# Reciprocals one product later in couples 6 to 9, and one weight sum in the other half of couple 10

## The chip, the core and the metric

The kernel runs on one core of a Trainium2 chip. Its time is the device time of one launch in microseconds; several launches give a median. The core has TensorE (PE in the profile, with its weight loads as PEld), VectorE (DVE), ScalarE (ACT), GpSimd (POOL) and SyncE (SP), which here only issues copies (DMAs). Each engine works through its own instructions in the order in which they were written; engines wait for each other through semaphores. TensorE writes into PSUM banks, and VectorE or ScalarE must empty a bank before TensorE can write the next result into it.

## The reference

Attention with normalised queries and keys (8 batches, 12 heads, 448 positions, 64 numbers per head) is followed by a feed-forward block with SiLU. All is fp32.

```python
q_n, k_n = rmsnorm(q, g_q), rmsnorm(k, g_k)
scores = matmul(q_n, k_n.T) / sqrt(64)
attn = exp(scores - max(scores)); attn /= sum(attn) + 1e-9
x = matmul(attn, v)            # arranged as 3584 tokens x 768
h = x @ w_in                   # 768 x 2048
out = (h * sigmoid(h)) @ w_out # 2048 x 768
```

## The kernel before, in words

The attention is worked off in 24 *couples* c = 0 to 23, each of two head pairs (four heads) of one batch. `GROUP` is 6 and `LATE` is 12. Each couple has a *visit* and a *between*.

**The visit.** `visit(c)` does the score matmuls of couple c (L712), the exponentials on ScalarE (L717), and the products with the values (`weigh`, L749), which gather unnormalised sums in two PSUM banks, `av0` and `av1`. The end of the weighing of couple c - 1 lies in visit c: after it, `divide(c - 1, sums)` (L808, VectorE) multiplies the two banks by the reciprocals r and writes x. Until that is done, the first `weigh` of couple c cannot start its new sums in these banks.

**The between.** `between(c)` prepares the next couple and, from couple 6 on, does a share of the first feed-forward matmul for the six couples (two batches) finished before. This share is the *filler*. It is dealt in two halves by `fill`: the first before, the second after the transposes of the next keys (L647) and the matmuls that sum the exponentials (L783). In couples 6 to 11 a half is 13 steps of one 128x128 by 128x448 matmul each.

**The filler's products.** The feed-forward matmul uses a seven-product scheme on 2x2 blocks (class `Seven`), with the order 1, 2, 6, 5, 7, 3, 4. A product is three steps into one bank (L907). After it the bank is emptied: products 2, 6, 7, 3 and 4 by a VectorE add (`plus`, L857), products 1 and 5 by a ScalarE copy (L915, L925). Between 7 and 3 GpSimd makes two adds: L927 adds product 5 to the term which product 3's emptying reads, and L928 makes another result. Two banks (`ps_mm`) take turns, so a product needs the bank of the last but one. When a block of seven is done, `activate` runs SiLU on its two rows (L1045, ScalarE) and SP saves them (L940). The generator of a product gives control back after each matmul, so the emptying of a product is written down when the next step is asked for.

**What `fill` interleaves.** `others` are spread evenly over the half's steps: normalising the next but one couple (L467 on ScalarE, L468 and L492 on VectorE, the power L496 on GpSimd), preparing `w_in` (below), and the adds L763 of the exponentials. `prompt` is a list with times of its own: its first entry is written before the first step, each further one after three more steps, which is one product. In the second half the prompt entries are the two halves of the reciprocal of the sums: `invert(0)`, and `invert(1)` with `spread`, L792 on VectorE. `spread` issues six copies on SP: four L799, then two L801, which overwrite what the first read and so wait until these have landed. They bring the reciprocals to where `divide` reads them. For couples 3 and 4 an empty entry stands ahead of the two, so that they come one product later.

**Preparing `w_in`.** Its four chunks are taken in pieces: SP loads raw words (L85), ScalarE opens them (L100, L101), VectorE rounds (L123, L126, L130) and GpSimd adds low bits (L134). The next load into a raw buffer waits for L134 of the piece that had it. Each finished chunk also needs four sums (`sum_w_in`, steps 0 to 3, L854 and L857 on tile W), which the products 5, 6, 7 and 3 read as weights. Those of the last chunk stand in the first half of couple 10 (entry 8 of `sums_halves`; the index is twice the couple's distance from `GROUP`, plus the half).

The instructions of each engine stand in the written order; nothing reorders them. SP works off its copies in order too, and one that waits holds up those behind it.

Of the kernel before, what the change touches and what calls it, by code (L numbers as in the profile page):

```python
# [535 lines left out]
def bounded(  # L536
# [13 lines left out]
    GROUP, LATE = z.NPAIR, z.LATE  # L550
# [13 lines left out]
    def piece(n):  # L564
        nonlocal at
        at += n
        return work[:, at - n : at]
# [71 lines left out]
    def transpose_k(c):  # L639


        assert z.KB == BANK
        t = ps.tile([P, 2, BANK], F32, name="sc", bufs=2)
        rows = place[f"k{c % 2}"]
        for i in range(2):
            for j in range(z.KEYS + 1 - i):
                nc.tensor.transpose(t[:, i, ts(j, P)], rows[:, ds((z.KA, z.KB)[i] + j * P, P)], ident)  # L647
        columns = t.rearrange("p i s -> p (i s)")[:, 0 : z.NK]
        nc.scalar.activation(kT, columns, AF.Copy, scale=gains)
        loads["k" if c < LATE - 1 else "quarters"](min(c + 2, LATE))  # L650

    def flip(c, name):

        if name == "q":
            nc.vector.transpose(qT.rearrange("p i s -> p (i s)"), q_of(c)[:, 0 : z.NK])
            load_q(c + 1)
            return
        nc.vector.transpose(kT, place["k1"])
        if c + 1 < NC:
            loads["quarters"](c + 1)  # L660
# [106 lines left out]
    def sum_up(c):  # L767

        n = D // 2
        early = c < GROUP
        t = bank(S) if c < GROUP - 1 else ps.tile([P, 2, BANK], F32, name="sc", bufs=2)[:, 0, 0:S]
        terms = [(0, lambda: weights(c, 0))]
        if early:
            terms = [(0, lambda: weights(c, LEFT - 1))] + terms + [(1, None)]
        for k, (which, w) in enumerate(terms):
            if k == len(terms) - 2:
                yield  # L780
            for h in range(2):
                for i in range(2):
                    nc.tensor.matmul(  # L783
                        t[ds(h * D + i * n, n), :],
                        ones[:, which + i if which else 0],
                        eleft[:, h] if which else w()[:, i, h],
                        start=(k == 0), stop=(k == len(terms) - 1),
                    )

        def invert(half):  # L790
            rows = ts(half, S // 2)
            nc.vector.reciprocal(out=r[0][:, rows], in_=t[:, rows])  # L792

        def spread():
            mine = [a.rearrange("(h i p) s -> i h p s", h=2, i=2) for a in r]
            queues = (nc.sync, nc.gpsimd if c == GROUP - 1 else nc.sync)
            for h in range(2):
                for i in range(2):
                    queues[h].dma_start(mine[1][i, h], mine[0][1, h])  # L799
            for h in range(2):  # L800
                queues[h].dma_start(mine[0][1, h], mine[0][0, h])  # L801

        yield [lambda: invert(0), lambda: (invert(1), spread())]

    def divide(c, source):
        for i in range(2):
            x = x_of(c, i)
            nc.vector.tensor_tensor(  # L808
                out=x, in0=x if source is None else source[i], in1=r[i], op=ALU.mult
            )  # L810
# [148 lines left out]
    def sum_w_in(i, step):  # L959

        assert room.w_in.rounded >= (i + 1) * z.NW
        summed.add((i, step))
        w = room.chunk(i).rearrange("p (c m r k) -> p c m r k", c=z.NW, m=2, r=2)
        up, low = w[:, 0:HW], w[:, HW:]
        s = room.sums(i).rearrange("p (s c m k) -> p s c m k", s=3, c=HW, m=2)
        left_sums(
            up[:, :, :, 0], low[:, :, :, 0], up[:, :, :, 1], low[:, :, :, 1],
            s[:, 0], s[:, 1], s[:, 2], (step,),
        )
# [8 lines left out]
    def sum_x(group, c, steps=range(4)):  # L978
        right_sums(*quarters(group, c), *sums_of_x(c), steps)
# [357 lines left out]
    def fill(others=(), prompt=()):  # L1337


        others, prompt, steps, dealt = list(others), list(prompt), 0, 0  # L1340
        if prompt:
            prompt.pop(0)()
        filler["due"] += filler["share"]
        total = max(1, int(filler["due"] / S))
        while filler["due"] > 0:
            step = next(filler["work"], None)
            if step is None:
                break
            filler["due"] -= step
            steps += 1  # L1350
            if prompt and steps % HW == 0:
                prompt.pop(0)()
            while dealt < min(len(others), len(others) * steps // total):
                others[dealt]()
                dealt += 1
        filler["due"] = min(filler["due"], 0.0)
        for other in prompt + others[dealt:]:
            other()
# [8 lines left out]
    def finish():  # L1367
        run(filler["work"])
# [10 lines left out]
    for c in range(GROUP // 2):  # L1379
        halves[2 * (c - GROUP)], halves[2 * (c - GROUP) + 1] = "rr", "o"  # L1380
    sums_halves = {-6: [(0, 0)], -4: [(0, 1)], -3: [(0, 2)], -2: [(0, 3)]}
    sums_halves[8] = [(3, step) for step in range(4)]
    sums_visits = {GROUP + 1: 1, GROUP + 3: 2}

    def weights_in(c, half):
        i = 2 * (c - GROUP) + half
        work = [step_of[step] for step in halves.get(i, "ro" if c < GROUP else "")]
        return work + [lambda a=a: sum_w_in(*a) for a in sums_halves.get(i, ())]
# [8 lines left out]
    def last_two(c):  # L1397
        return [c // GROUP * 2 - 2, c // GROUP * 2 - 1]
# [63 lines left out]
    def run_all(work):  # L1462
        for piece in work:
            piece()

    def between(c):

        def transposes_and_sums():
            summing = sum_up(c)
            if c < GROUP:  # L1470
                next(summing)
            if c == GROUP - 1:
                reciprocals = next(summing)
                divide(c - 1, None)
                run_all(reciprocals)
                sum_x([0, 1], 0)
                transpose_k(c + 1)
                return
            if c < LATE - 1:
                transpose_k(c + 1)  # L1480
            reciprocals = next(summing)
            if LATE - 1 <= c < NC - 1:
                reciprocals += [lambda: flip(c + 1, "k"), gain]
            if GROUP // 2 <= c < EARLY:
                divide(c - 1, None)
            return reciprocals

        if c < LATE - 1:
            transpose_q(c + 1)
        elif c < NC - 1:  # L1490
            flip(c + 1, "q")
        if c < GROUP // 2:
            inverting.extend(transposes_and_sums())
        elif c == GROUP - 1:
            transposes_and_sums()
        if c >= GROUP and c % GROUP == 0:
            fetched = range(AHEAD) if c == GROUP else ()
            columns = products - 2 * HW * S * len(fetched)
            work = halves_in(last_two(c), range(HF), plain_in, dict(begun), fetched)
            begin(work, columns, 2 * GROUP)  # L1500
            begun.clear()
        late = add(c, LEFT - 1) + add(c, LEFT) if c >= GROUP else []
        further = normalise(c + 2) if c >= GROUP - 1 else []
        fill(late + weights_in(c, 0) + (further[2:] if c >= GROUP else further[:2]))
        prompt = transposes_and_sums() if GROUP // 2 <= c != GROUP - 1 else []
        if prompt and c < GROUP:
            prompt.insert(0, lambda: None)
        if c == GROUP // 2:
            begin(make_ahead([0, 1]), AHEAD * 2 * HW * S, GROUP - 1)
        if c >= LATE - 2:  # L1510
            if c == LATE - 2:
                prompt.append(pair_up)
            queries = prompt[3:] + [lambda: sum_squares(c + 2)]
            fill(weights_in(c, 1), prompt[:3] + [lambda: run_all(queries)])
        else:
            fill(weights_in(c, 1) + (further[:2] if c >= GROUP else []), prompt)
        if c % GROUP == GROUP - 1:
            finish()
            if c == GROUP - 1:
                begun[0] = fetch_ahead([0, 1], 0)  # L1520
            elif c < NC - 1:
                sum_x([c // GROUP * 2, c // GROUP * 2 + 1], 0, range(2))
        if c >= LATE - 2:
            scale(c + 2)
        if GROUP <= c < NC - 1:

            nc.scalar.activation(first, minus_half, AF.Exp)
        if c == NC - 1:
            while rounder.load():
                pass  # L1530
# [238 lines left out]
```

## Time and profile before

| | us |
|---|---|
| median of three launches | 1319.01 (1318.58 to 1319.05) |
| profiled execution, its own time | 1321.49 |
| profiled execution, span | 1319.7 |
| PE busy | 1296.1 |
| DVE busy | 951.2 |
| ACT busy | 505.5 |
| POOL busy | 361.6 |

Couples 6 to 10 lie between about 123 and 297 us of the span. Rows of the timeline give the start in us from the span's start, the duration, the engine, the line and operation, output and inputs, the number of instructions merged, and in brackets how long the engine had stood idle before and what released it. On TensorE each matmul is two records in this profile, so a product of three matmuls is "x6". A duration on TensorE holds the time in the pipeline too: the starts of neighbouring rows say how fast work proceeds.

### The profile page before, as it was taken

Reading aid. Unit: us, or ns where it says so; the run is one execution under the profiler, and the core shown is the slowest. Engines: PE = TensorE matmul, PEld = TensorE weight load, DVE = VectorE, ACT = ScalarE, POOL = GpSimd, SP = SyncE. Lnnn points to the kernel's source line nnn. Section 1 sums busy time; section 2 is a strip of 40 time slices with the busy share of each in tenths; the row PEclk is TensorE's granted clock in tenths of the full one; section 3 lists DMA queues with packets and bytes.
Section 4 is the critical chain, followed back from the end, with each engine's and each line's share of the span. In section 5 each row is a group of like instructions: output and inputs, shape, how many; then the busy total and the mean of one; then the engine's idle time right before and its main releaser. Section 6 shows DMA issues by size and latency. Waiting matters only on the chain.

```text
span 1319.7 us, 19838 instructions
## 1 busy us (share of the span) xinstructions
PE 1296.1 (98%) x7193; PEld 829.9 (63%) x7193; DVE 951.2 (72%) x1629; ACT 505.5 (38%) x886; POOL 361.6 (27%) x230
## 2 busy tenths in 40 slices
PE   8989999999999999999999999999999999999998
PEld 4433444444444444444444455558999999999998
DVE  6888776785755555855554686698978787878785
ACT  7956555654555555454544244410100000000000
POOL 6756533343334333433420244410000000000000
PEclk9999999999999999999999999999999999999999
DMA  8664336333444444444321367412323232231311
GB/s 228 171 174 128 113 91 195 89 90 86 97 103 109 99 93 118 98 93 118 84 64 67 111 201 258 143 60 76 101 76 106 78 100 97 84 117 61 132 45 39
DMA packets 249439, 144.94 MB, mean 110 GB/s; under 512 B 184292, under 2 KB 233220, under 8 KB 249332
## 3 DMA queue, kind: packets, MB, share of 16 engines
q1 hardware_dynamic: 248672, 142.42, 38.6%
q8 instruction: 59, 0.97, 0.3%
q0 software_dynamic: 352, 0.96, 0.2%
q14 instruction: 48, 0.39, 0.1%
q10 hardware_dynamic: 308, 0.20, 0.1%
HBM read 93.98 MB, written 41.29 MB: 102 GB/s over the span
## 4 chain that ended last, share of the span: by engine, by line
PE 87%; DVE 5%; ACT 3%; issue 2%; DMA 2%; POOL 1%; SPq 0%; ACTq 0%; DVEq 0%; POOLq 0%
PE alone L1214 23%; PE mm L907 19%; PE sc L907 9%; PE av L749 8%; PE mm L1214 8%; PE sc L712 8%; PE alone L907 7%; PE alone L1251 2%; PE sc L783 1%; ACT work L717 1%; DMA work<-work 1%; PE mm L1251 1%; DVE work L792 1%; DVE work L763 1%; DMA hidden<-stage 1%
## 5 line engine op out<-in xcount | busy, mean ns | idle before, releaser
L717 ACT ACTIVATE work<-sc,rms 128x448 f32<-128x448 f32 x324 | 185.0, 634 | 70.1 <-PE sc L712 53.5
L907 PE MATMUL mm<-x,W 128*128 128x448 f32 x414 | 169.5, 544 | 3.0 <-DVE stage L857 1.6
L712 PE MATMUL sc<-work 64*64 64x448 f32 x1344 | 165.4, 548 | 1.8 <-ACT work L717 1.5
L763 DVE TENSOR_TENSOR work<-work 128x896 f32<-128x896 f32 (+1 forms) x114 | 123.7, 1118 | 50.7 <-PE av L749 45.4
L749 PE MATMUL av<-work,rows 64*64 64x448 f32 x1296 | 152.8, 541 | 2.9 <-ACT av L725 2.2
L907 PE MATMUL mm<-sums_x,W 128*128 128x448 f32 x372 | 152.5, 543 | 1.9 <-DVE parts L857 1.9
L496 POOL TENSOR_TENSOR rms<-rms,minus_half 128x14 f32<-128x14 f32 (+4 forms) x43 | 105.2, 2449 | 150.6 <-DVE rms L492 140.8
L907 PEld LDWEIGHTS mm<-x,W 128*128 128x128 f32 x414 | 76.6, 190 | 86.2 <-issue 75.5
L523 POOL DMA_DIRECT2D out_dram<-x x2 | 1.2, 594 | 443.3 <-DVE x L857 443.3
L907 PEld LDWEIGHTS mm<-sums_x,W 128*128 128x128 f32 x372 | 69.2, 190 | 75.2 <-issue 67.6
L1214 PE MATMUL alone<-W,rows 128*128 128x192 f32 x610 | 113.0, 326 | 0.0
L749 PEld LDWEIGHTS av<-work,rows 64*64 64x64 f32 x1296 | 57.7, 132 | 75.2 <-issue 34.8
L1214 PEld LDWEIGHTS alone<-W,rows 128*128 128x128 f32 x610 | 101.4, 190 | 0.0
L712 PEld LDWEIGHTS sc<-work 64*64 64x64 f32 x1344 | 53.0, 133 | 75.2 <-ACT work L717 30.7
L927 POOL TENSOR_TENSOR parts<-parts,stage 128x448 f32<-128x448 f32 x31 | 42.1, 1357 | 147.9 <-DVE parts L857 147.7
L907 PE MATMUL sc<-x,W 128*128 128x448 f32 x198 | 80.6, 543 | 0.0
L688 POOL TENSOR_TENSOR rms<-rms,minus_half 128x28 f32<-128x28 f32 x12 | 57.5, 4793 | 61.4 <-DVE rms L685 54.8
L1214 PE MATMUL alone<-W,work 128*128 128x192 f32 x382 | 72.2, 326 | 0.0
L1045 ACT ACTIVATE stage<-stage 128x896 f32<-128x896 f32 x63 | 57.3, 945 | 21.9 <-DVE stage L857 21.1
L1224 ACT COPY rows<-alone 128x192 f32<-128x192 f32 x33 | 10.5, 319 | 142.1 <-PE alone L1214 78.4
L468 DVE TENSOR_REDUCE rms<-rows 128x8 f32<-128x512 f32 (+2 forms) x56 | 35.9, 641 | 39.1 <-ACT rows L467 37.9
L1214 PEld LDWEIGHTS alone<-W,work 128*128 128x128 f32 x382 | 63.8, 190 | 0.0
(258 smaller groups left out, 2276.7 us busy)
## 6 DMA issues: line engine op xcount, KB each, us to landing
hidden<-stage SPq DMA_DIRECT2D x63, 448.0 KB, 3.1
work<-hidden SPq DMA_DIRECT2D x21, 1024.0 KB, 5.0
rows<-in_moe_w_out_dram SPq DMA_DIRECT2D x32, 384.0 KB, 3.4
W<-in_moe_w_in_dram SPq DMA_DIRECT2D x22, 512.0 KB, 5.4
work<-work SPq DMA_DIRECT2D x141, 56.0 KB, 2.0
x<-hidden SPq DMA_DIRECT2D x7, 1024.0 KB, 5.6
rows<-in_q_dram SPq DMA_DIRECT2D x96, 56.0 KB, 2.2
rows<-in_k_dram SPq DMA_DIRECT2D x96, 56.0 KB, 2.2
```

What stands on the lines that cost most here:

```text
L468: nc.vector.tensor_reduce(out=out, in_=t.rearrange("p (n d) -> p n d", n=n), axis=AX.X, op=ALU.add)
L496: nc.gpsimd.tensor_tensor(out=t, in0=t, in1=half, op=ALU.pow)
L688: nc.gpsimd.tensor_tensor(out=f, in0=f, in1=minus_half.to_broadcast([P, n]), op=ALU.pow)
L712: nc.tensor.matmul(two[ds(half * D, D), h, 0:S], keys[rows, ts(half, D)], qT[rows, pair, :], start=True, stop=True,)
L717: nc.scalar.activation(eleft[:, h] if j == LEFT else weights(c, j)[:, i, h], two[:, h, 0:S], AF.Exp, scale=norm.column(c, i, h, j),)
L749: nc.tensor.matmul(sums[i][ds(h * D, D), :], v, w, start=(j == 0 and step == 1), stop=(j == LEFT - 1 and step == 1),)
L763: nc.vector.tensor_tensor(out=total, in0=total, in1=more, op=ALU.add)
L907: nc.tensor.matmul(t, self.left(name, s), self.right(name, s), start=s == ends[0], stop=s == ends[1])
L927: nc.gpsimd.tensor_tensor(out=u2, in0=u2, in1=p5, op=ALU.add)
L1045: nc.scalar.activation(t, t, AF.Silu)
L1214: nc.tensor.matmul(t, x[:, i], y, start=i == ORDER[0], stop=i == ORDER[-1])
L1251: nc.tensor.matmul(o, a[:, 2 * i + m, t], right_one(name, i)[:, m], start=n == 0, stop=n == len(steps) - 1,)
```

## The change

It has three parts.

1. The empty entry ahead of the reciprocals is now put in for couples up to 9 and not only up to 5: `c < LATE - 2` in place of `c < GROUP`. In couples 6 to 9 the first half of the reciprocal is written after the first product's worth of steps of the second half, and the second half, with the spread's copies, after the second.
2. In couple 10 the first half of the filler gets three sums of the last chunk of `w_in`, and the second half the fourth.
3. In couples 10 and 11 the second half's `others` are now this list followed by as many empty entries. In couple 10 the fourth sum is thereby dealt about halfway through; in couple 11 the list is empty, as before.

```diff
-    sums_halves[8] = [(3, step) for step in range(4)]
+    sums_halves[8] = [(3, step) for step in range(3)]
+    sums_halves[9] = [(3, 3)]
...
-        if prompt and c < GROUP:
+        if prompt and c < LATE - 2:
             prompt.insert(0, lambda: None)
...
             queries = prompt[3:] + [lambda: sum_squares(c + 2)]
-            fill(weights_in(c, 1), prompt[:3] + [lambda: run_all(queries)])
+            steps = weights_in(c, 1)
+            fill(steps + [lambda: None] * len(steps), prompt[:3] + [lambda: run_all(queries)])
```

The built programs hold the same instructions. Their order is the same on PE, ACT and POOL. On VectorE, in couples 6 to 9, a product's emptying now precedes the first half of the reciprocal; in couples 6, 7 and 9 the second half follows the rounding of a piece of `w_in` (and in couple 6 another emptying), and in couple 8 it follows product 3's emptying and precedes the rounding. In couple 10 the three emptyings of the first half stand one instruction earlier among the adds L763 and the weight sums. On SP the six copies of the spread move behind a weight load and two saves in couple 6, and behind two saves in couple 9.

## The prediction

> **What bounds the kernel now.** The page comes first: TensorE is busy nearly all of the span, so only stretches in which it stands idle can be won, and each new wait of TensorE costs its full length.
>
> ```profile
> span 1319.7 us, 19838 instructions
> ...
> PE 1296.1 (98%) x7193; PEld 829.9 (63%) x7193; DVE 951.2 (72%) x1629; ACT 505.5 (38%) x886; POOL 361.6 (27%) x230
> ```
>
> The timeline of TensorE gives the start of each couple (the first score matmuls of its visit): couple 7 at 157.43, 8 at 191.65, 9 at 227.22, 10 at 260.54, 11 at 297.23. So the stretches from 7 to 11 take 34.2, 35.6, 33.3 and 36.7 us. The stretch of couple 9 has no idle product and is my measure of "clean". Products elsewhere that start late:
>
> ```profile
> 183.93 4.78 PE L907 MATMUL mm<-x,W 128*128 128x448 f32 x12 [0.62 <-ACT stage L925]
> ...
> 219.85 2.52 PE L907 MATMUL mm<-sums_x,W 128*128 128x448 f32 x6 [1.58 <-DVE parts L857]
> ...
> 281.81 2.52 PE L907 MATMUL mm<-x,W 128*128 128x448 f32 x6 [0.90 <-DVE stage L857]
> ```
>
> A product runs 2.25 us (4.51 between two starts two products apart, rows x12). Measured from start to start, these three cost 0.9, 2.25 with its two small followers at 222.33 and 224.76, and 1.07 us. They are waits for one of the two product banks, which VectorE or ScalarE has yet to empty. In couple 8 the emptying stands behind a reciprocal, and the next one behind GpSimd:
>
> ```profile
> 217.77 1.55 DVE L792 RECIPROCAL work<-sc 128x224 f32<-128x224 f32 x1
> 219.24 0.56 DVE L857 TENSOR_TENSOR parts<-mm,parts 128x448 f32<-128x448 f32 x1
> 219.72 1.54 DVE L792 RECIPROCAL work<-sc 128x224 f32<-128x224 f32 x1
> 221.65 0.62 DVE L857 TENSOR_TENSOR stage<-mm,parts 128x448 f32<-128x448 f32 x1 [0.39 <-POOL parts L927]
> ...
> 224.09 0.62 DVE L857 TENSOR_TENSOR stage<-mm,parts 128x448 f32<-128x448 f32 x1
> ```
>
> ```profile
> 217.94 2.58 POOL L496 TENSOR_TENSOR rms<-rms,minus_half 128x14 f32<-128x14 f32 x1 [4.67 <-DVE rms L492]
> 220.48 1.13 POOL L927 TENSOR_TENSOR parts<-parts,stage 128x448 f32<-128x448 f32 x1
> ```
>
> The page's chain of waits puts 87% on PE and 5% on DVE, in line with this.
>
> What a later reciprocal must not delay is the spread: six copies on SP that bring the reciprocals to all partitions, and the division that frees the weighted sums' banks. In couple 6, SP issues them right after the second reciprocal, ahead of a weight load and two saves; the division then ends just as TensorE wants the bank:
>
> ```profile
> 151.45 2.47 SPq L799 DMA_DIRECT2D work<-work  x4
> 154.14 1.72 SPq L801 DMA_DIRECT2D work<-work  x2
> 155.96 0.52 SPq L85 DMA_DIRECT2D W<-in_moe_w_in_dram  x1
> 156.57 0.86 SPq L940 DMA_DIRECT2D hidden<-stage  x2
> ```
>
> ```profile
> 161.49 1.16 DVE L808 TENSOR_TENSOR x<-av,work 128x448 f32<-128x448 f32 x2 [1.31 <-PE av L749]
> ```
>
> ```profile
> 162.78 0.93 PE L749 MATMUL av<-work,rows 64*64 64x448 f32 x8
> ```
>
> [...] L799 lands in a median of 2.0 us, but behind a 512 KB load the first pair kept L801 waiting:
>
> ```profile
> 82.09 0.65 SPq L85 DMA_DIRECT2D W<-in_moe_w_in_dram  x1
> 82.84 2.66 SPq L799 DMA_DIRECT2D work<-work  x4
> 88.31 1.14 SPq L801 DMA_DIRECT2D work<-work  x2
> ```
>
> That is 5.5 us from first L799 to first L801, where couple 6 has 2.7. [...] the L927 add takes 1.97 us at 278.44 beside VectorE's adds and 1.13 at 220.48.
>
> **The change part by part.** [...] I take times in the old frame and let each couple shift what follows.
>
> *Couple 7.* The emptying of the product before (ended 179.04) now precedes the first reciprocal: it goes at 182.01 instead of 183.48. The bank is free at 182.6; TensorE starts at 183.04 instead of 183.93. Behind it on VectorE: reciprocal to 184.05, rounding 1.45 to 185.5, reciprocal to 187.0, emptying at 187.0 to 187.5, when TensorE's next bank is wanted (187.55). Gain 0.9. The spread starts at 187.05 instead of 185.53; its 6.3 us (first issue to landing: 2.7 + 1.8 + 1.9) end at 193.4, the division is at about 194.9: hidden.
>
> *Couple 8.* Product 7 is emptied at 217.77 and its successor starts at 218.4, 1.45 earlier. But product 3's emptying needs L927, which stays behind the 2.58 us L496 and ends at 221.61 as before; VectorE waits from 219.8, because the second reciprocal now stands behind that emptying. So the product after still starts at 222.33, the reciprocal runs 222.2 to 223.7, rounding to 225.1, product 4's emptying to 225.7 instead of 224.7. TensorE starts its last product at 225.75 instead of 224.76: cost 1.0, and the 1.58 won is all given back.
>
> *Couple 9.* Nothing waits today; the second reciprocal ends at 257.25 instead of 255.05, and the emptying behind it slips 0.3 from 256.94, wanted only at 258.95. But SP now issues the two saves (ready at 257.4 and 258.3) before the spread: it starts at 258.85 instead of 255.16, its first pair lands about 262.2 behind 896 KB, and all about 264.6. The division is at 264.60 today and TensorE has 1.4 more: cost 0, between 0 and 0.6. Queued behind the division are two roundings and the adds of couple 10.
>
> *Couple 6.* Emptying at 149.1, reciprocal to 151.1, rounding to 152.6, emptying to 153.1, reciprocal to 154.6. Within the half this gains 0.2 (the product at 153.48 stood 0.2 to 0.3 for its bank). On SP the weight load waits for GpSimd's L134 after the rounding (1.29 us, to about 154.05), then 0.5 for its issue and 0.9 for the saves: the spread's first copy leaves at 155.6 instead of 151.45. Ahead of it lie 512 + 896 KB; today they take 6.6 us from the load's issue to the last save's landing (155.96; 157.0 + 5.6), so now until 160.7. The first pair lands about 161.0, the last two copies go to 162.2, r is there at 163.7. Division 163.7 to 164.9; TensorE, which could take up to 0.5 of delay on the second bank (wanted at 163.15), waits for 164.9: cost 1.8. Bounds: 0 if small copies pass the big ones, 3.6 if r comes as late as the slowest landing in the trace (6.9 us for L799) makes it. [...] Next late are only VectorE's sums after the division, with 0.99 and 2.32 us of idle before they are missed.
>
> *Couple 10.* Its first half has VectorE without a pause. The fourth sum (1.1 us) leaves it, and the order puts the emptying at 277.69 before the fifth add, and the next, at 281.14, before the first weight sum, which today costs it 1.77: it moves to 279.3. The wait of 1.07 goes; TensorE would want that bank at 280.74. The half ends 1.1 earlier, VectorE 1.4; a 0.1 wait at 290.64 goes too. The fourth sum runs at 290.2 in the second half, where VectorE has 2.6 us idle before 295.46; its reader is the product at 296.14. Gain 1.2; not under 0.5, not over 1.6.
>
> Sum: -0.2 + 1.8 - 0.9 + 1.0 + 0 - 1.2 = **+0.5 us**, on the profiled execution's 1321.49 (1.8 around its span), 0.2% above the median; on the median of 1319.01 it gives 1319.5.
>
> **Rivals.** (a) *The waits go and nothing takes their place*: 0.9 + 2.25 + 1.2, or 4.3 faster, 1314.7. For it: the rows name the emptyings that move; against it: L496 and L927 do not move. (b) *Small copies pass*: the sum without the 1.8 of couple 6: 1317.7. Against it: the row at 88.31. (c) *Slower: the spread behind the saves decides.* In couple 6 it costs 3.6, and couple 9's r comes 1.5 late, so VectorE reaches the emptying in couple 10 0.6 too late: -0.2 + 3.6 - 0.9 + 1.0 + 0.1 - 0.6 = +3.0, 1322.0. It decides once r arrives after 165 in couple 6. For it: 1.4 MB stand ahead; against it: at 297.34, behind 896 KB, the delay was only 1.3. (d) *The order does not reach the chip*: excluded, the built order differs.
>
> **How the numbers follow.** Forecast 0.5 (own range 1317.9 to 1321.3), (a) 0.12, (b) 0.13, (c) 0.25. Range 1316.0 to 1322.6: it leaves out (a) and the outer end of (c). 0.2% is 2.6 us, about what a measurement can tell from no change. Faster: (a) and 0.03 from elsewhere, 0.15. Slower: 0.2 of (c) and 0.05 of the forecast, 0.25. The rest, 0.60, is within.
>
> **What would show it.** Couple starts: the stretch 7 to 8 should be some 0.9 longer (+1.8 - 0.9), 8 to 9 longer by 1.0, 9 to 10 unchanged, 10 to 11 shorter by 1.2. In couple 6 SP should show L85, L940, then L799, a gap of over 4 us from first L799 to first L801, and the division waiting for a DMA. In couple 8 VectorE should idle 1.8 us for L927. If the division of couple 6 still waits for TensorE, or L927 runs before 219.5, I am wrong.

## The result, and the profile after

| | before | after |
|---|---|---|
| median, us (13 launches each) | 1319.69 (1318.58 to 1323.01) | 1323.15 (1319.85 to 1326.73) |
| profiled execution, its own time | 1321.49 | 1322.69 |
| profiled execution, span | 1319.7 | 1320.9 |

The ratio is 1.0025, with a 95% interval of 1.0017 to 1.0032. That is 2.2 to 4.2 us slower, where the prediction had 0.5; 1323.15 lies 0.55 above the upper end of its range.

Couple by couple, from the starts of the score matmuls on TensorE's timeline (156.69, 192.19, 228.85, 262.17, 298.55 and 330.51 for couples 7 to 12):

| stretch | before | after | difference | predicted |
|---|---|---|---|---|
| second half of couple 6 | 11.81 | 11.71 | -0.10 | -0.2 |
| 7 to 8 | 34.22 | 35.50 | +1.28 | +0.9 |
| 8 to 9 | 35.57 | 36.66 | +1.09 | +1.0 |
| 9 to 10 | 33.32 | 33.32 | 0 | 0 |
| 10 to 11 | 36.69 | 36.38 | -0.31 | -1.2 |
| 11 to 12 | 31.96 | 31.96 | 0 | 0 |

The sum is +1.96. The spans differ by less, 1.2, because the profiled execution of after came to the second half of couple 6 0.64 earlier, ahead of anything that the change touches. So this execution of after shows about 2 of the 3.3 us of the ratio. The rest was found later, in other executions.

The group of the value products on the page of before, then the page of after, its head and the same group:

```profile
L749 PE MATMUL av<-work,rows 64*64 64x448 f32 x1296 | 152.8, 541 | 2.9 <-ACT av L725 2.2
```

```profile
span 1320.9 us, 19844 instructions
...
PE 1298.5 (98%) x7193; PEld 832.6 (63%) x7193; DVE 946.0 (72%) x1629; ACT 504.8 (38%) x886; POOL 360.1 (27%) x230
...
L749 PE MATMUL av<-work,rows 64*64 64x448 f32 x1296 | 154.9, 544 | 5.1 <-DVE x L808 2.6
```

TensorE has the same 7193 matmuls; L749 now waits 2.6 us for the division L808, in two places (1.05 in visit 6, 1.57 in visit 7). How the one in visit 7 comes about is seen on SP's timeline in couple 6 (start, time of issuing, then the copies merged in the row):

```profile
153.60 0.33 SPq L85 DMA_DIRECT2D W<-in_moe_w_in_dram  x1
154.03 0.86 SPq L940 DMA_DIRECT2D hidden<-stage  x2
154.98 3.71 SPq L799 DMA_DIRECT2D work<-work  x4
160.45 1.14 SPq L801 DMA_DIRECT2D work<-work  x2
```

The load and both saves now go ahead of the spread, and its two steps stand 5.5 us apart (154.98 to 160.45), where before had 2.7. VectorE's timeline of after, with the division of couple 6 in its first row and the second half of couple 8 below:

```profile
163.11 1.16 DVE L808 TENSOR_TENSOR x<-av,work 128x448 f32<-128x448 f32 x2 [3.67 <-DMA work<-work]
...
218.38 0.62 DVE L857 TENSOR_TENSOR parts<-mm,parts 128x448 f32<-128x448 f32 x1
218.91 1.55 DVE L792 RECIPROCAL work<-sc 128x224 f32<-128x224 f32 x1
222.25 0.62 DVE L857 TENSOR_TENSOR stage<-mm,parts 128x448 f32<-128x448 f32 x1 [1.79 <-POOL parts L927]
222.79 1.55 DVE L792 RECIPROCAL work<-sc 128x224 f32<-128x224 f32 x1
...
225.72 0.62 DVE L857 TENSOR_TENSOR stage<-mm,parts 128x448 f32<-128x448 f32 x1
```

The division used to wait for TensorE; it now waits 3.67 us for a DMA. In couple 8 the first emptying is early, and VectorE then idles 1.79 us for GpSimd's L927, with the second reciprocal queued behind. GpSimd, in the same place:

```profile
218.54 2.58 POOL L496 TENSOR_TENSOR rms<-rms,minus_half 128x14 f32<-128x14 f32 x1 [4.74 <-DVE rms L492]
221.09 1.12 POOL L927 TENSOR_TENSOR parts<-parts,stage 128x448 f32<-128x448 f32 x1
```

TensorE's timeline of after, in couples 7, 8, 10:

```profile
160.50 1.72 PE L712 MATMUL sc<-work 64*64 64x448 f32 x16
163.79 1.13 PE L749 MATMUL av<-work,rows 64*64 64x448 f32 x6 [1.57 <-DVE x L808]
...
184.58 4.67 PE L907 MATMUL mm<-x,W 128*128 128x448 f32 x12
...
219.05 2.52 PE L907 MATMUL mm<-sums_x,W 128*128 128x448 f32 x6 [0.23 <-DVE parts L857]
222.93 2.52 PE L907 MATMUL mm<-x,W 128*128 128x448 f32 x6 [1.35 <-DVE stage L857]
226.39 1.77 PE L907 MATMUL mm<-x,W 128*128 128x448 f32 x4 [0.95 <-DVE stage L857]
...
283.12 2.52 PE L907 MATMUL mm<-x,W 128*128 128x448 f32 x6
```

Against before: from the scores at 160.50 to the products at 163.79 it is 3.29 us, where it was 1.54, so the stall costs 1.75. The waits of the products in couple 7 (184.58) and in the first half of couple 10 (283.12) are gone. The row of before put the one in couple 7 down to ScalarE's L925. It was VectorE's emptying: in after, L925 begins at 184.78, when the product (184.58) already runs. In couple 8 the wait of 1.58 has become 0.23, and the next two starts (222.93, 226.39) wait 1.35 and 0.95 instead.

### The profile page after: what moved, and what is told of

It is laid out like the page before. It is cut to its first block, busy times and chain, and to the rows that moved or that the text cites. A ratio compares the mean times of both kernels' runs of the same rounds, so it can differ in the third digit from the quotient of the medians.

```text
span 1320.9 us, 19844 instructions
## 1 busy us (share of the span) xinstructions
PE 1298.5 (98%) x7193; PEld 832.6 (63%) x7193; DVE 946.0 (72%) x1629; ACT 504.8 (38%) x886; POOL 360.1 (27%) x230
## 4 chain that ended last, share of the span: by engine, by line
PE 88%; DVE 4%; ACT 3%; issue 2%; DMA 2%; POOL 1%; SPq 0%; ACTq 0%; DVEq 0%; POOLq 0%
PE alone L1214 23%; PE mm L907 20%; PE sc L907 9%; PE av L749 8%; PE mm L1214 8%; PE sc L712 8%; PE alone L907 7%; PE alone L1251 2%; PE sc L783 1%; DMA work<-work 1%; ACT work L717 1%; DVE work L792 1%; PE mm L1251 1%; DMA hidden<-stage 1%; PE sc L629 1%
## 5 line engine op out<-in xcount | busy, mean ns | idle before, releaser
L763 DVE TENSOR_TENSOR work<-work 128x896 f32<-128x896 f32 (+1 forms) x114 | 124.6, 1125 | 51.7 <-PE av L749 51.1
L749 PE MATMUL av<-work,rows 64*64 64x448 f32 x1296 | 154.9, 544 | 5.1 <-DVE x L808 2.6
L496 POOL TENSOR_TENSOR rms<-rms,minus_half 128x14 f32<-128x14 f32 (+4 forms) x43 | 105.2, 2449 | 148.7 <-DVE rms L492 138.5
L749 PEld LDWEIGHTS av<-work,rows 64*64 64x64 f32 x1296 | 58.0, 133 | 79.3 <-issue 36.1
L927 POOL TENSOR_TENSOR parts<-parts,stage 128x448 f32<-128x448 f32 x31 | 41.9, 1350 | 148.9 <-DVE parts L857 148.7
L792 DVE RECIPROCAL work<-sc 128x224 f32<-128x224 f32 x38 | 58.6, 1547 | 6.4 <-PE sc L783 6.2
```

What stands on the lines that cost most here:

```text
L496: nc.gpsimd.tensor_tensor(out=t, in0=t, in1=half, op=ALU.pow)
L749: nc.tensor.matmul(sums[i][ds(h * D, D), :], v, w, start=(j == 0 and step == 1), stop=(j == LEFT - 1 and step == 1),)
L763: nc.vector.tensor_tensor(out=total, in0=total, in1=more, op=ALU.add)
L927: nc.gpsimd.tensor_tensor(out=u2, in0=u2, in1=p5, op=ALU.add)
```

## The experiments

The theory from the two traces: couple 6 loses at the division, because the spread stands behind the load and the saves on SP; couple 8 loses because L496 holds L927 and with it the second reciprocal; couples 7 and 10 gain what the prediction said. Rivals: the six copies are late because the reciprocals themselves are, not because of what is ahead of them; couple 9 costs more than it shows; and the 1.3 us that the stretches of one execution don't show are a cost outside of couples 6 to 10, or one that is there in some executions only. Ratios are to the kernel before, run on the same chip; its medians there were 1320.2 (first four), 1320.5 (next four) and 1319.7 us (last four). The intervals of the ratios are 1.8 to 2.9 us wide, so for a single couple the stretch in the trace is the finer measure. The stretch 8 to 9 alone varies where nothing in it was changed, from 35.38 to 35.83.

### One couple at a time

Each of four kernels delays the reciprocals in one couple alone, and leaves the sums where they were (N is 6, 7, 8 or 9):

```diff
-        if prompt and c < GROUP:
+        if prompt and (c < GROUP or c == N):
```

> The empty entry is added for couple 6 alone. Theory (the spread's copies wait on SP behind one weight load and two saves): the division of couple 6 waits for its reciprocals, TensorE for the division; 1.3 us slower than before (0.2 gained within the half, 1.5 lost). Rival (the stall also costs a window of half TensorE clock afterwards, which would explain why the changed kernel lost 3.3 us where its trace shows under 2): 2 to 3.5 us slower, with a mean granted clock lower than that of before. Rival (the reciprocals' own place on VectorE is what costs): the same 1.3, but with the division waiting for VectorE and not for a copy.

> The empty entry is added for couple 7 alone. Theory: the product after the keys' transposes no longer waits for its bank; 0.9 us faster than before, at most 1.1. Rival (the gain is only moved to a later wait, as in couple 8): no change, within 0.3 us.

> The empty entry is added for couple 8 alone. Theory (GpSimd's power L496 ahead of L927 holds product 3's emptying, and the second reciprocal behind that delays product 4's): 1.0 us slower than before, and VectorE idle 1.8 us ahead of product 3's emptying. Rival (the first wait of 1.6 us is simply removed): 1.5 to 2.2 us faster.

> The empty entry is added for couple 9 alone. Theory after the result (the spread stands behind two saves on SP and the division comes over a microsecond late): 0.7 to 1.7 us slower, since TensorE waits at the weighing in visit 10 and VectorE, which has no pause in the first half of couple 10, comes later to its emptyings there (that half's fourth weight sum is still in it, so the late division is not cushioned). The forecast on record: between 0 and 0.6 us slower.

| kernel | ratio, interval | the stretch concerned, before and now |
|---|---|---|
| couple 6 alone | 1.0025 (1.0014 to 1.0036) | 7 to 8: 34.22, 38.03 |
| couple 7 alone | 0.9994 (0.9986 to 1.0003) | 7 to 8: 34.22, 33.34 |
| couple 8 alone | 1.0008 (1.0000 to 1.0016) | 8 to 9: 35.57, 36.50 |
| couple 9 alone | 1.0007 (0.9998 to 1.0016) | 10 to 11: 36.69, 37.15 |

Couple 7 gains 0.88, couple 8 loses 0.93, couple 9 loses 0.46, all near what the whole change showed; the intervals of couples 7 and 9 hold 1, so the evidence for these two is the stretch. Couple 6 alone, though, costs 3.81 in its stretch and 3.3 us by the ratio: as much as the whole change. In the whole change's trace it can only have cost 1.28 + 0.88 = 2.16 of that stretch. TensorE's timeline of couple 6 alone shows what comes on top:

```profile
163.37 1.41 PE L749 MATMUL av<-work,rows 64*64 64x448 f32 x6 [1.66 <-DVE x L808]
164.24 0.96 PE L712 MATMUL sc<-work 64*64 64x448 f32 x2
```

The two matmul records of such a row took 0.54 us in the changed kernel (at 164.59) and take 0.96 here. The table of stretches tells why; its columns are the stretch, its length, busy time of PE, PEld, DVE, ACT and POOL, the granted TensorE clock, the busy share of the DMA engines and GB/s. First couple 6 alone, then the changed kernel:

```profile
163.00:167.00 4.00, 3.63 (x22) 2.13 (x26) 3.96 (x6) 0.23 (x1) 0.00 (x0) 0.64 0.14 32
```

```profile
163.00:167.00 4.00, 3.21 (x30) 1.86 (x32) 3.86 (x6) 1.56 (x4) 0.27 (x1) 1.00 0.23 52
```

After the stall the granted clock is 0.5 for 3.41 us (from 164.09 on; the mean over 163 to 167 is 0.64). By an estimate from these two numbers that costs half of 3.41 us, 1.7 us; the difference of the two stretches, 3.81 - 2.16 = 1.65, agrees. In the first profile of the changed kernel the stall was followed by a clock of 1.00.

### The spread ahead of the load and the saves, in couple 6

In couple 6 the emptyings keep their new order, but the load and the two saves that the change puts ahead of the spread are held back until it is issued:

```diff
-        if prompt and c < GROUP:
+        if prompt and (c < GROUP or c == 6):
             prompt.insert(0, lambda: None)
+            if c in (6,):
+                hold_back()
+                prompt.append(let_go)
```

`hold_back` makes the load and `save` only note that they were called; `let_go`, one product after the spread, issues them.

> Couple 6 alone as before, but the weight load and the two saves of that half are held back on SP until the spread's six copies have been issued (as they stand in the kernel before). Theory (it is the place behind 1.4 MB on SP that makes the reciprocals late, not their place on VectorE): the first L801 follows the first L799 by 2.7 us again, the division waits for TensorE, and the time is that of before or 0.2 us less. Rival (the reciprocals' later end by 3.2 us is enough): still 1.5 us or more slower than before.

The ratio is 1.0001 (0.9992 to 1.0010), and the stretch 7 to 8 takes 34.20 us, as before. The timelines of this kernel, SP and then VectorE:

```profile
154.34 2.47 SPq L799 DMA_DIRECT2D work<-work  x4
157.02 1.72 SPq L801 DMA_DIRECT2D work<-work  x2
158.85 0.52 SPq L85 DMA_DIRECT2D W<-in_moe_w_in_dram  x1
```

```profile
160.91 1.16 DVE L808 TENSOR_TENSOR x<-av,work 128x448 f32<-128x448 f32 x2 [1.31 <-PE av L749]
```

The copies leave 2.52 us ahead of the start of visit 7 (156.86 here), where the changed kernel has 1.71 and before 5.98: they are nearly as late as in the changed kernel. But L801 follows after 2.7 us and not after 5.5, and the division waits for TensorE again. So the reciprocals are not too late in themselves: what stood ahead of their copies decides.

One more kernel holds back the saves alone and lets the load go ahead, so that 512 KB stand ahead of the spread and not 1.4 MB (the same edit without the part on the load):

> Couple 6 alone with the empty entry; only the two saves are held back until the spread is issued, the 512 KB weight load stays ahead of it. Theory [...]: the first L801 follows the first L799 by 3 to 4 us, r is there about 162, the division is at most 0.6 late, TensorE waits at most 0.3, and the time is within 0.5 us of before; no window of half clock after it. Rival (the load's own wait for GpSimd is what delays the spread): 1.5 us or more slower.

The ratio is 1.0000 (0.9990 to 1.0009), the stretch 34.28. Its timelines of SP and VectorE:

```profile
151.78 0.33 SPq L85 DMA_DIRECT2D W<-in_moe_w_in_dram  x1
152.35 2.48 SPq L799 DMA_DIRECT2D work<-work  x4
156.50 1.14 SPq L801 DMA_DIRECT2D work<-work  x2
```

```profile
159.18 1.16 DVE L808 TENSOR_TENSOR x<-av,work 128x448 f32<-128x448 f32 x2 [1.57 <-DMA work<-work]
```

With 512 KB ahead, L801 follows after 4.15 us. The division does wait for the copies, but it comes only some 0.25 later in its visit than before (4.31 us after the visit's start against 4.06). Its stretch is 0.06 longer than before. So the load alone costs next to nothing, and the loss comes only with the 896 KB of saves on top of it; the saves without the load were not tried. The landings follow the order on SP: the first L799 landed 0.2 us after the load where only that stood ahead of it (156.24 against 156.04), and 0.2 us after the second save in the changed kernel (160.26 against 160.08). The traces of before and of the changed kernel show the landing of 639 of SP's copies each, and in both every one of these landed at least 0.15 us after the one of them issued before it.

### GpSimd's power behind L927, in couple 8

Couple 8 alone, with the power L496 of that half written after the two adds L927 and L928 and after L134 (it belongs to the keys of couple 10, which are normalised in couple 8):

```diff
-                norm.root(c, name)
+                norm.root(c, name, put_off=powers if name == "k" and c == 10 else None)
...
+            if name == "q":
+                while powers:
+                    powers.pop()()
...
-        if prompt and c < GROUP:
+        if prompt and (c < GROUP or c == 8):
```

> Couple 8 alone has the empty entry, and GpSimd's power L496 of that place, whose result is wanted only two couples later, comes after L927 and L928 instead of before. Theory (L496 is what turned the gain of couple 8 into a loss): product 3's emptying comes about 1.8 us earlier, and the couple is 0.5 to 0.9 us faster than in the kernel before, where couple 8 alone without this was 1.1 slower. Rival (the reciprocals' order on VectorE itself costs the 1.1): still slower than before.

The ratio is 0.9992 (0.9985 to 1.0000), against 1.0008 for couple 8 without this; the stretch 8 to 9 takes 34.61 us, 0.96 less than before and 1.89 less than couple 8 alone. GpSimd and VectorE of this kernel (here the emptying is L865, the reciprocal L795, L927 is L935 and L496 is L497):

```profile
215.51 1.14 POOL L935 TENSOR_TENSOR parts<-parts,stage 128x448 f32<-128x448 f32 x1 [5.23 <-ACT W L100]
...
221.63 2.60 POOL L497 TENSOR_TENSOR rms<-rms,minus_half 128x14 f32<-128x14 f32 x1
```

```profile
214.75 0.62 DVE L865 TENSOR_TENSOR parts<-mm,parts 128x448 f32<-128x448 f32 x1
215.28 1.55 DVE L795 RECIPROCAL work<-sc 128x224 f32<-128x224 f32 x1
216.75 0.56 DVE L865 TENSOR_TENSOR stage<-mm,parts 128x448 f32<-128x448 f32 x1
217.23 1.55 DVE L795 RECIPROCAL work<-sc 128x224 f32<-128x224 f32 x1
```

VectorE's wait of 1.79 us is gone and the two reciprocals run without a pause. That shows that the power held L927, and L927 the rest. One wait of 0.63 us for a bank is left on TensorE in the stretch, behind the second reciprocal and the rounding.

### The sums of couple 10 alone

```diff
-    sums_halves[8] = [(3, step) for step in range(4)]
+    sums_halves[8] = [(3, step) for step in range(3)]
+    sums_halves[9] = [(3, 3)]
...
-            fill(weights_in(c, 1), prompt[:3] + [lambda: run_all(queries)])
+            steps = weights_in(c, 1)
+            fill(steps + [lambda: None] * len(steps), prompt[:3] + [lambda: run_all(queries)])
```

> The fourth weight sum alone moves into the second half of couple 10; the reciprocals stay where they were. Theory: the wait of about 1 us in the first half of couple 10 goes and none comes in the second; 1.0 to 1.2 us faster than before. Rival (the wait turns up again at the end of the couple, where TensorE waits for a bank whose emptying waits for a save): within 0.3 us of before.

The ratio is 0.9991 (0.9984 to 0.9998), the stretch 10 to 11 takes 35.82, 0.87 less. Of the forecast 1.2, the wait in the first half is gone. The wait near the end of the couple is not; before and this kernel alike have it at 0.72 us (the row of this kernel):

```profile
293.51 1.02 PE L907 MATMUL mm<-x,W 128*128 128x448 f32 x2 [0.72 <-DVE parts L857]
```

### The whole change, with the spreads ahead in couples 6 and 9

The whole change and the holding back of above for couples 6 and 9:

```diff
+            if c in (6, 9):
+                hold_back()
+                prompt.append(let_go)
```

> The whole change, with the spread issued ahead of the weight load and the saves in couple 6, and ahead of the saves in couple 9. Theory (these two places cost 1.5 and 0.7 us directly, and the rest of the 3.3 us is the window of half TensorE clock that follows the stall of couple 6 in some executions): no window after the stall, and 1.0 us faster than before (-0.2, -0.9, +1.1, 0, -1.0). Rival (the change costs what it costs for other reasons): 2 us or more slower than before.

The ratio is 0.9993 (0.9982 to 1.0004): nothing is left of the 1.0025. The stretches are 33.33 (7 to 8: couple 7's gain alone), 36.61 (8 to 9, couple 8's loss) and 35.83 (10 to 11). The last one was 36.38 in the changed kernel, so couple 9's spread cost 0.55 there. SP's timeline of the changed kernel in couple 9:

```profile
259.08 1.18 SPq L940 DMA_DIRECT2D hidden<-stage  x2
260.35 2.61 SPq L799 DMA_DIRECT2D work<-work  x4
263.38 3.02 SPq L801 DMA_DIRECT2D work<-work  x2
```

And VectorE's, where the division waited for TensorE before:

```profile
267.94 1.16 DVE L808 TENSOR_TENSOR x<-av,work 128x448 f32<-128x448 f32 x2 [2.92 <-DMA work<-work]
```

The first L801 goes after 3.0 us, about as the prediction had it, but the second only at 265.9. It waited for the last L799, which was issued at 262.4 and took 3.5 us, although the saves had landed by 262.9. The same copy took 3.3 us in couple 9 alone and 3.6 in a second execution of the changed kernel, against 2.0 in before, so it is no accident of one execution. Why it took so long stays open.

### The kernels with couple 6's stall once more

Half a clock behind couple 6's stall was the one cost that the changed kernel's first trace did not have. The changed kernel and couple 6 alone were each profiled in one more execution, with no edit.

> The kernel with the empty entry in couple 6 alone, looked at once more. Theory (the stall in visit 7 brings a window of half TensorE clock in most executions): a window of 3.41 us again shortly after the stall. Rival (the window of the first look was chance): none.

> The changed kernel, looked at once more. Theory: a window of 3.41 us at half clock shortly after the stall of visit 7, absent from its first profile, and the stretch from couple 7 to couple 8 longer by 1.7 us than there. Rival: none, as in the first profile.

They took 1324.58 (couple 6) and 1324.51 us (the change), and both have the half clock. TensorE's timeline of the changed kernel in this second execution, and its stretch:

```profile
163.29 1.43 PE L749 MATMUL av<-work,rows 64*64 64x448 f32 x6 [1.80 <-DVE x L808]
164.20 0.96 PE L712 MATMUL sc<-work 64*64 64x448 f32 x2
```

```profile
163.00:167.00 4.00, 3.71 (x22) 2.19 (x26) 3.97 (x6) 0.00 (x0) 0.00 (x0) 0.62 0.13 28
```

Compared with the first execution of the same kernel, the stretch 7 to 8 is 37.29 and not 35.50 us, 1.79 more: 0.23 of it is a longer stall, 1.56 the clock. The sum over the stretches from 7 to 11 is +4.2 instead of +2.1, and the 3.3 us of the ratio (3.5 by the medians) lies between, nearer to the upper one. Of the four profiles in which the load and both saves go first in couple 6, three have the half clock there (two of couple 6 alone, one of the change); of the ten profiles without that order (before and nine kernels), none has.

A stall of this length doesn't always bring it, and the traces show on what that depends. Visit 6, which the change doesn't touch, has a stall of 1.97 us (to 0.01) in all 14 profiles. In before it was followed by half a clock (TensorE's timeline, then the table of stretches, cut where the clock changes):

```profile
123.70 1.21 PE L749 MATMUL av<-work,rows 64*64 64x448 f32 x8 [1.97 <-ACT av L725]
```

```profile
120.92:124.33 3.41, 1.44 (x20) 0.40 (x16) 3.38 (x5) 1.88 (x5) 1.07 (x2) 1.00 0.10 23
124.33:127.74 3.41, 3.41 (x20) 0.80 (x12) 3.34 (x7) 1.97 (x4) 3.29 (x2) 0.50 0.65 150
```

In the profile of couple 8 alone it was not:

```profile
121.35 0.98 PE L749 MATMUL av<-work,rows 64*64 64x448 f32 x8 [1.97 <-ACT av L725]
```

```profile
117.69:121.11 3.42, 1.70 (x20) 0.46 (x12) 3.35 (x6) 1.86 (x4) 0.64 (x2) 1.00 0.06 17
121.11:124.52 3.41, 2.49 (x24) 0.82 (x24) 3.31 (x7) 2.97 (x8) 3.29 (x2) 1.00 0.51 117
```

These stretches lie on a grid. In every trace with several spells of half clock, the times at which they set in are whole multiples of 3.413 us apart: in before 73.13, 124.33 and 1315.58 us (15 and 364 multiples of it after the first), in the first execution of the changed kernel 72.27, 123.47 and 1318.14 (15 and 365), in its second 123.02 and 163.97 (12). So one spell is taken to give the grid of a whole execution (couple 8 alone has its only one at 1315.77, 350 multiples after 121.11). Where the grid lies against the kernel differs from one execution to the next: visit 6's stall ends 0.63 us ahead of a grid time in before (123.70), 1.21 ahead in the first execution of the changed kernel (122.26), 0.24 behind one in couple 8 alone (121.35). In before the whole stall falls into one interval of the grid, and the next interval is at half clock. In couple 8 alone it is cut in two, 1.71 and 0.25 us, and nothing follows. Over the 14 profiles this stall fell into one interval nine times, and half a clock followed nine times; it was cut in two five times, and the interval after neither part was slowed by it.

All intervals of the 14 traces between 30 and 1300 us that ran at full clock say the same, 5187 in number. With 1.97 us or more of TensorE idle (15 intervals) the next one was always at half clock; with 1.59 us or less (5165) never; between 1.66 and 1.87 us (7) three times. In before the longest idle times of an interval were 2.67, 1.97 and 1.58 us, and only the first two were followed by half a clock; in the first execution of the changed kernel 2.01, 1.98 and 1.57, with the same outcome. Behind an interval already at half clock less was seen to be enough: in visit 6 of four profiles one with 0.42 to 1.00 us of idle time was followed by another. Couple 6's stall fell into one interval in all four profiles: its 1.66, 1.80 and 1.86 us brought the half clock, and the 1.57 us of the changed kernel's first profile did not. The idle times rest on modelled ends of matmuls, so the limit is not exact, and what decides between 1.66 and 1.87 us stays open.

### A version of the parts that gained

Couples 7 and 8 with the late reciprocals, the power of couple 8 behind L927, and the sums moved; couples 6 and 9 as before:

```diff
-        if prompt and c < GROUP:
+        if prompt and (c < GROUP or c in (7, 8)):
```

(with the edits of "GpSimd's power behind L927" and "The sums of couple 10 alone").

> Of the change only what gained is kept: the empty entry in couples 7 and 8, with GpSimd's power of couple 8 after L927 and L928, and the fourth weight sum in the second half of couple 10. Couples 6 and 9 stay as before. Theory (the parts add): 0.8 + 1.0 + 1.2, or 3.0 us faster than before. Rival (gains of neighbouring couples overlap, since a bubble removed early only lets TensorE run into the next): 1 to 2 us faster.

The ratio is 0.9977 (0.9968 to 0.9986), or 3.0 us faster than before; the medians, 1317.69 and 1319.7, differ by 2.0. The stretches from 7 to 11 are 33.32, 34.80, 33.32 and 35.82, together 2.5 shorter than before. The single ratios of its three parts give -0.8, -1.1 and -1.2, together -3.1, and their stretches -2.7.

## Why the prediction was wrong, step by step

The parts add up: the ratios of couples 6, 7, 8, 9 and the sums alone give +3.3 - 0.8 + 1.1 + 0.9 - 1.2 = +3.3 us, which is the whole change's. That they agree so closely is in part luck, since each has an interval of some 2 us or more. Beside the forecast (+1.6 with the gain within the half, -0.9, +1.0, 0, -1.2) couple 6 misses by 1.7, couple 9 by 0.9 (0.5 by its stretch), the others by 0.1 at most. So each step can be looked at by itself.

- **Couple 7**, forecast -0.9: right. The wait for VectorE's emptying is gone, the stretch is 0.88 shorter, and the spread was hidden. (The spread's 2.7 + 1.8 + 1.9 add up to 6.4 and not to 6.3; with over a microsecond to spare it makes no difference.)
- **Couple 8**, forecast +1.0: right, in mechanism and in size (0.93 alone, 1.09 in the change; VectorE's idle time of 1.79 us was forecast as 1.8). That L496 ahead of L927 makes the loss was shown by moving it: the couple then gains 0.96.
- **Couple 10**, forecast -1.2: the wait in the first half went as foreseen, and the gain is 0.87. The 1.07 read from start to start was too much: alone, the product starts 0.88 earlier in its couple (20.39 us after the start of visit 10 instead of 21.27), as the 0.90 of idle time in the row said. The 0.1 expected at a later product brought nothing. In the whole change the stretch shows -0.31, because couple 9's late spread takes 0.55 of it.
- **Couple 9**, forecast 0, with 0 to 0.6 as bounds: mis-sized. The traces give 0.46 to 0.55. The order of the copies on SP was foreseen, that the last L799 takes 3.5 us was not: the last reciprocals landed 5.6 us after the visit's start (267.81 - 262.17), where the forecast had 4.1 (264.6 - 260.54).
- **Couple 6**, forecast +1.8 at the division and -0.2 within the half: this is the step that failed, though its mechanism was right as far as the stall. SP's order, the gap of over 4 us and the division's wait for a DMA came as foreseen, and the reciprocals landed 6.3 us after the visit's start (162.99 - 156.69), which is the forecast's time (163.7 - 157.43). That the spread lands behind what was issued ahead of it was read from the row at 88.31, and the landings (160.08 and 160.26) bear it out. The stall itself was 1.75 us, and the half gained 0.1. But the part costs 2.16 in its stretch without the half clock, since the rest of the visit loses another 0.4 (not taken apart), and 3.81 with it. What failed is the opening sentence of the prediction, that each new wait of TensorE costs its full length. It put the clock afterwards at nothing; this stall cost its length and, in three of four profiles, half a clock for 3.41 us besides (1.65 and 1.56 us in two of them, by their stretches).

The trace of before could have warned of this: behind the stall of 1.97 us in visit 6 the granted clock is 0.50 from 124.33 to 127.74. The link from the stall to the half clock is shown by where it occurs, three times out of four behind couple 6's stall (1.66, 1.80 and 1.86 us within one interval, not 1.57) and never at that place without it, and by the stall of visit 6, which brought it the nine times that it fell into one interval and not once in the five that it was cut in two. Why TensorE's clock is halved was not shown.

Rival (c) forecast a total of +3.0, close to what was measured, but for another reason: it had couple 6 cost 3.6 by the division alone and couple 10's gain halved because couple 9's reciprocals come 1.5 late. The first did not come about (1.75 of stall, with the clock on top); that the totals agree is luck. The second did: the reciprocals were 1.6 late and the loss was 0.55. But it arises in visit 10: the last sixteen products of `weigh` start there 10.13 us after the visit's start in the changed kernel and 9.43 in before, so the loss is made ahead of the emptying that (c) named. Rivals (a) and (b) are out: the bank waits were replaced in couple 8, and the small copies did not pass.

## What to carry to other kernels

Keep small copies that something urgent waits for ahead of bulk loads and saves on the same queue: before moving work that issues copies, list what they end up behind (here 1.4 MB, with which L801 followed 5.5 us after L799 and not 2.7). Price a new TensorE stall of some 1.7 us or more as its length plus, with some chance (three of four profiles here), half of the 3.41 us that the clock was at half, by estimate 1.7 us. Look in the trace for stalls of that length already there and at the clock behind them. One execution may not show this cost, as the changed kernel's first did not, so profile several. Emptying a bank earlier gained 0.88 us in couple 7 and lost 0.93 in couple 8, where the next emptying was held 1.79 us by another engine; in such a place, move what holds it (here a power of 2.6 us on GpSimd, after which couple 8 gained 0.96) as well.

## What the runs showed that was not expected

- TensorE's clock was halved in spells that began on a grid of 3.413 us. In these traces an interval at full clock with at least 1.97 us of idle time was always followed by one at half clock (15 of 15), one with at most 1.59 us never (0 of 5165). A stall of 1.97 us that the grid cut in two (five profiles) brought nothing.
- The delay of six copies of 56 KB behind bulk on one queue: 2.7 us from first L799 to first L801 with nothing ahead, 4.15 behind a 512 KB load, 5.5 behind that and 896 KB of saves.
- One such copy took 3.5 us in couple 9, though the saves ahead of it had landed 0.6 us after its issue (3.3 and 3.6 us in two other profiles); its cause is open.
